# Gate magnitudes from the ratio, and transposes in front of `up` in two row tiles, in a gated linear attention followed by a low-rank mixer

## The chip, the core and the metric

The kernel runs on one core of one Trainium2 chip. A core has a matrix engine (TensorE, PE in the profile, with its weight loads shown apart as PEld), a vector engine (VectorE, DVE), an activation engine (ScalarE, ACT), GpSimd (POOL) and a queue engine (SyncE, SP). They run side by side, each through its own instructions in order, and wait for each other through semaphores. PE writes to PSUM only, and DVE or ACT copy from there. DMA engines move data between the chip's main memory and the core's; here the loads are issued by SP and most of the stores by POOL. The metric is the time of one execution on the device, in microseconds (us); smaller is better.

## The reference

Two stages. The first is a linear attention with complex gates: B = 4 batches, H = 8 heads, S = 768 steps, head size D = 48.

```python
mag = np.sqrt(a_re * a_re + a_im * a_im)
scale = np.minimum(mag, 0.999) / (mag + 1e-06)
a_re_n, a_im_n = (a_re * scale, a_im * scale)
for t in range(S):
    ar, ai = (a_re_n[:, :, t, :, None], a_im_n[:, :, t, :, None])
    new_re = ar * S_re - ai * S_im
    new_im = ar * S_im + ai * S_re
    kv = np.einsum('bhd,bhe->bhde', k[:, :, t], v[:, :, t])
    S_re, S_im = (new_re + kv, new_im)
    y[:, :, t] = np.einsum('bhd,bhde->bhe', q[:, :, t], S_re)
```

Its output, heads side by side (x, 4 x 768 x 384), goes through a mixer: a product of rank 32 over the steps, then two channel products with a hidden size of 1536.

```python
xt = x.transpose(0, 2, 1)
h = xt @ U @ V
u = x + h.transpose(0, 2, 1)
ch = np.maximum(u @ w_ch1, 0.0) @ w_ch2
return (u + ch).astype(np.float32)
```

The weights of the mixer arrive in float64; q, k, v and the gates in float32.

## The kernel before, in words

The steps are cut into 24 chunks of 128 (six for each batch). In a chunk the recurrence becomes products: with the running log magnitude and the running phase of the gates, q and k are weighted by exp and by cosine and sine, and then a masked product within half chunks and a state between them give y.

**Gates.** Two chunks form a group (`GROUPS`, 12 groups of 128 x 768 values; group 0 is done in two parts of 384). `magnitudes_of` (L644) squares both parts of the gate on ACT (L651), adds them with bounds on DVE (L654), keeps a bounded sum (L655), and checks on DVE with two maxima (L657) whether the real part is larger than the imaginary one in size. ACT takes a Ln, an Exp and a Ln (L660 to L662); then the log magnitude with its cap comes either from DVE alone (L665, L667; groups 0 to 2, `SPREAD`) or from an ACT Relu and DVE (L669, L670). From group 3 on (`SPLIT`) the result `GL` is split into two reduced-precision halves `GS` (L676, L677). A second Ln and Exp give one over the magnitude, and its product with the imaginary part (L680) is the ratio whose arc tangent is the angle (after the magnitude's part, L718). `within` (L684) forms the prefix sum over the steps on PE (`es ps`, L691 and L695) and two Exp of it (`es`). `angles` does the same for the phase (`ph`, L755 to L761; the rounding to whole turns is `F`, L763 and L764), `waves` gives cosine and sine (`cs`). Ln and Exp are in one table of ACT, arc tangent and sine in another; a change is a table load (L435).

**Chunks.** `prep` (L793) weights q and k on DVE (L801), multiplies them with `cs` (L805, `QKC`), and turns the result on PE: 16 transposes of 64 rows each, in two row tiles of the array (`tile_position`, L816), whose results ACT copies to `QK` (L822). `chain` (L827) has the inner products (L845), their mask (L848), the state (`dk`, L865) and the output (`y`, L894 and L902), whose copies give `xo` (L911, L913).

**Mixer.** `mixer` (L918) works on pairs of chunks: `rank` (L937), `mixed` (L960), then `turned` (L969): three whole 128 x 128 transposes of u for each chunk (`uTp`, L976) and one copy to `uT`, on DVE for the first chunk of a pair (L982) and on ACT for the second (L980). The first channel product is `up` (L991) for the first two pairs and from the third pair on `up_fewer` (`few`, L1103), a scheme with 15 block products instead of 18. The second is `down` (L1192) for the first pair and `down_two` (L1235, 7 instead of 8 block products) for the others. Stores follow (`leave`, L1179). The weights are turned from float64 into float32 by five steps of DVE or ACT for each block of 768 columns (`single`, L555), with two buffers for the raw words, so the third block is loaded only when the first or the second has been converted.

**What sets the order.** Every step is entered with `plan.add`, which numbers it. The list `ORDER` gives the order in which the numbered steps are issued; each engine's queue has its own steps in that order. `reads` and `writes` of a step only serve to refuse an order in which a step comes before what it needs. `SPARE` names steps in front of which filler matmuls are issued. PSUM has two pools: `psM` with 2 tiles, used by `up`, `down` and parts of `few`, and `psS` with 6 for everything else.

At the end `judge` (L1361) counts on PE whether any of the checks failed; if so, a general version of the kernel runs (`in_general`), which with these inputs it does not.

## Time and profile before

| | |
|---|---|
| time, median of 3 runs | 555.85 us (555.32 to 556.29) |
| profiled execution, from its first to its last instruction | 552.8 us |
| the median less that span: what lies around it | 3.05 us |
| PE busy | 526.9 us (95%) |
| weight loads busy | 477.3 us (86%) |
| DVE busy | 432.8 us (78%) |
| ACT busy | 317.8 us (57%) |
| POOL busy | 32.2 us (6%) |
| read from main memory, written | 33.60 MB, 4.76 MB |

The profile is of one execution, and its time is told as the span alone; the whole time of that execution is not among its rows, so the last line of the three sets it against the median of the runs. "Busy" is the time in which an engine has an instruction in work; PE's instructions overlap, so a busy PE is not yet PE at its peak. In rows by group, the numbers after the bar are the sum of busy time and the mean duration of one instruction in ns, and after the next bar the idle time of the engine in front of them with what ended it. In the chain of waits each line is a piece of the chain that ended last, with its start, its length and what ran.

### The profile page before, as it was taken

The numbers are of one execution on the slowest core, as the hardware profiler recorded it, in microseconds if no ns is written. First come the engines' busy times: TensorE is split into PE (matmuls) and PEld (weight loads), VectorE is DVE, ScalarE is ACT, GpSimd is POOL, SyncE is SP. The second block draws the span as 40 slices with busy tenths as digits, with TensorE's granted clock in tenths as the row PEclk, the third lists the DMA queues.
The fourth block names the chain that finished last, engine by engine and source line by source line (L and its number), as shares of the span: only waits on it lengthen the run. The fifth ranks groups of instructions, "written<-read, shape, count | busy, mean of one in ns | idle before, by whom it ended". The sixth has DMA issues, their size and how long they took to land.

```text
span 552.8 us, 16672 instructions
## 1 busy us (share of the span) xinstructions
PE 526.9 (95%) x7228; PEld 477.3 (86%) x7228; DVE 432.8 (78%) x828; ACT 317.8 (57%) x553; POOL 32.2 (6%) x61
## 2 busy tenths in 40 slices
PE   2899999999999999999999999999999999999996
PEld 1677776767999987999999998999999989999995
DVE  6899989999999987998787987786953635567352
ACT  6889999795597787567827956626512232110100
POOL 1000000001010000102001001002000000000000
PEclk9999999999999999999999999999999999999999
DMA  9988876523441354314513425003300000000001
GB/s 229 187 184 174 195 170 151 144 30 87 88 89 30 56 104 77 59 31 85 91 38 67 74 38 111 2 1 59 59 9 23 17 11 15 8 8 23 21 9 34
DMA packets 150688, 39.92 MB, mean 72 GB/s; under 512 B 145912, under 2 KB 147408, under 8 KB 150608
## 3 DMA queue, kind: packets, MB, share of 16 engines
q1 hardware_dynamic: 148400, 34.43, 31.2%
q0 software_dynamic: 2208, 4.35, 2.3%
q8 instruction: 59, 0.97, 0.7%
q14 instruction: 21, 0.17, 0.1%
HBM read 33.60 MB, written 4.76 MB: 69 GB/s over the span
## 4 chain that ended last, share of the span: by engine, by line
PE 73%; DVE 12%; ACT 4%; issue 2%; DMA 1%; POOL 0%; DVEq 0%; SPq 0%; ACTq 0%; POOLq 0%
PE down L1235 26%; PE few L1103 25%; PE tr L816 4%; PE dk L865 3%; PE inner L845 3%; PE y L902 3%; PE up L991 2%; PE y L894 2%; DVE xo L444 1%; ACT gate L438 1%; PE rank L937 1%; PE ph L755 1%; PE mixed L960 1%; PE uTp L976 1%; PE es ps L691 1%
## 5 line engine op out<-in xcount | busy, mean ns | idle before, releaser
L1111 ACT COPY h<-few 128x512 f32<-128x512 f32 x60 | 35.1, 585 | 87.3 <-PE few L1103 87.1
L1235 PE MATMUL down<-w,h 128*128 128x192 f32 x396 | 72.7, 330 | 0.9 <-DVE xo L444 0.7
L438 ACT ACTIVATE gate<-gate 128x768 f32<-128x768 f32 (+2 forms) x74 | 65.6, 900 | 9.2 <-DVE GS L750 3.8
L1235 PEld LDWEIGHTS down<-w,h 128*128 128x128 f32 x396 | 64.5, 190 | 3.7 <-issue 1.5
L822 ACT COPY QK<-tr 112x512 f32<-112x512 f32 x96 | 49.9, 596 | 17.8 <-PE tr L816 17.7
L444 DVE TENSOR_TENSOR xo<-down,xo 128x192 f32<-128x192 f32 (+1 forms) x79 | 29.9, 385 | 33.9 <-PE down L1235 33.4
L1115 DVE CUSTOM_DVE_ANT_1 h<-few,h 128x512 f32<-128x512 f32 x60 | 40.5, 686 | 15.7 <-PE few L1103 11.8
L1103 PE MATMUL few<-extra,w 128*128 128x128 f32 x400 | 50.9, 276 | 0.0
L1103 PEld LDWEIGHTS few<-extra,w 128*128 128x128 f32 x400 | 48.0, 192 | 0.1
L441 DVE TENSOR_TENSOR QKC<-qk,cs 128x768 f32<-128x768 f32 x48 | 44.4, 950 | 1.7 <-PE dk L865 1.3
L1235 PE MATMUL down<-stage 128*128 128x192 f32 x198 | 37.9, 330 | 0.4 <-DVE xo L444 0.4
L438 ACT ACTIVATE es<-es ps 128x384 f32<-128x384 f32 x48 | 20.1, 502 | 31.2 <-PE es ps L691 29.2
L444 DVE TENSOR_TENSOR h<-few,h 128x512 f32<-128x512 f32 x30 | 20.6, 688 | 20.4 <-ACT h L1111 12.1
L1179 POOL DMA_DIRECT2D out_dram<-xo x32 | 17.9, 558 | 313.8 <-DVE xo L444 297.7
L991 PE MATMUL up<-uT,w 128*128 128x256 f32 x144 | 34.5, 387 | 0.7 <-ACT uT L980 0.7
L1235 PEld LDWEIGHTS down<-stage 128*128 128x128 f32 x198 | 32.3, 190 | 1.7 <-DVE xo L444 1.0
L1103 PE MATMUL few<-gate,w 128*128 128x128 f32 x240 | 32.2, 278 | 0.4 <-DVE gate L1075 0.4
L435 ACT ACT_TABLE_LOAD x24 | 30.8, 1283 | 1.1 <-PEq L1439 0.7
L816 PEld LDWEIGHTS tr<-ident,QKC 64*112 64x112 f32 x768 | 24.2, 130 | 8.3 <-issue 3.6
L816 PE MATMUL tr<-ident,QKC 64*112 64x64 f32 x768 | 28.9, 221 | 2.4 <-DVE QKC L441 2.4
L991 PEld LDWEIGHTS up<-uT,w 128*128 128x128 f32 x144 | 26.4, 190 | 5.3 <-ACT uT L980 0.9
L1103 PEld LDWEIGHTS few<-gate,w 128*128 128x128 f32 x240 | 29.3, 192 | 0.8 <-PE uTp L976 0.6
(161 smaller groups left out, 1100.4 us busy)
## 6 DMA issues: line engine op xcount, KB each, us to landing
stage<-in_moe_w_ch_dram SPq DMA_DIRECT2D x12, 768.0 KB
gate<-in_a_im_dram SPq DMA_DIRECT2D x24, 192.0 KB
gate<-in_a_re_dram SPq DMA_DIRECT2D x24, 192.0 KB
VP<-in_v_dram SPq DMA_DIRECT2D x24, 192.0 KB
qk<-in_q_dram SPq DMA_DIRECT2D x24, 192.0 KB
qk<-in_k_dram SPq DMA_DIRECT2D x24, 192.0 KB
out_dram<-xo POOLq DMA_DIRECT2D x12, 192.0 KB, 2.2
out_dram<-xo POOLq DMA_DIRECT2D x20, 96.0 KB, 2.1
```

Source lines behind the costliest of these rows:

```text
L435: ACT(1.4, rank, lambda: nc.scalar.preload_act_table_set(name), writes=[TABLE])
L438: return nc.scalar.activation(out=o, in_=i, func=f, **kw)
L441: nc.vector.tensor_tensor(out=o, in0=a, in1=b, op=OP.mult)
L444: nc.vector.tensor_tensor(out=o, in0=a, in1=b, op=OP.add)
L816: nc.tensor.transpose(out=get(*ps[r])[0:DQ, h], in_=get(*qkc)[at, h].rearrange("p u d -> p (u d)")[:, 0:DQ], identity=ident[at, at], tile_ ...
L822: nc.scalar.copy(out=get(*QK)[:, u].rearrange("p (h t) -> p h t", t=CH)[:, :, r * HC:(r + 1) * HC], in_=get(*ps[r])[0:DQ])
L991: nc.tensor.matmul(out=get(*ps)[:, e], lhsT=w1[:, f, (ff + e) * 128:(ff + e + 1) * 128], rhs=get(*uT)[:, f], start=(f == 0), stop=(f == KD ...
L1103: nc.tensor.matmul(out=get(*ps)[:, q], lhsT=w()[:, q * 128:(q + 1) * 128], rhs=v[0](), start=(n == 0 and q == 0), stop=True, skip_group_ch ...
L1111: ACT(c_act(n3 * CH) - 0.045, RU, lambda i=i, k=k: nc.scalar.copy(out=at(i, k), in_=get(*ps)), [ps], [o])
L1115: DVE(c_dve(n3 * CH), RU, lambda i=i, k=k: nc.vector._custom_dve(dve_ops.TENSOR_ADD_SAT, out=at(i, k), in0=get(*ps), in1=at(i, k), s0=math ...
L1179: queue.dma_start(out=out[b, c * CH:(c + 1) * CH, lo:hi], in_=get("xo", i)[:, lo:hi])
L1235: nc.tensor.matmul(out=get(*to)[:, part], lhsT=x(j), rhs=y[:, j], start=(first and j == 0), stop=(j == KH - 1), skip_group_check=not first)
```

## The change

There are four parts.

1. For the groups from 1 on (`RATIO`) `magnitudes_of` hands over to a new `ratio_of`. It bounds the real part from below by a tiny number, takes Ln of it and Exp of minus that (one over the real part), multiplies by the imaginary part (the ratio), squares that on DVE with a running maximum (`wide`, the check that the ratio is at most 1 in size), and takes Ln of 1 plus the square. The negative log magnitude is then minus half of this less the Ln of the real part; Exp and Ln for the 1e-6 and the cap follow. Squares, bounded sums, the two maxima and the second Ln and Exp are gone in these groups. The split is moved into a function of its own, unchanged. Group 0 stays as it was.
2. `turned` makes six transposes of 64 rows in two row tiles, into two PSUM tiles, and copies each half on its own, one on DVE and one on ACT. For the last two pairs these PSUM tiles come from the pool `psM`.
3. Reads and writes of some steps in the plan are changed (`w2i`, `bank`, the whole of `y[1]`). They bind the order and add no instruction. `judge` has one more column to reduce, to compare and to count.
4. `ORDER` is another list throughout (2203 steps instead of 2210), and `SPARE` has 31 filler steps instead of 34.

```diff
 SPARE = {
-    125: 2, 135: 10, 199: 14, 209: 1, 223: 5, 243: 2,
+    125: 2, 135: 10, 196: 14, 220: 5,
 }
...
+    RATIO, TINY = 1, 2.0 ** -60
...
-    low = singles.tile([128, GC * DM], FP, name="low")
+    low = singles.tile([128, DM], FP, name="low")
...
-    bad = singles.tile([128, 1 + 2 * NT], FP, name="bad")
+    bad = singles.tile([128, 1 + 2 * GC], FP, name="bad")
     nc.vector.memset(bad, -1.0)
+    wide = singles.tile([128, 1 + NG], FP, name="wide")
+    nc.vector.memset(wide, 0.0)
...
+            if g >= RATIO:
+                ratio_of(lo, hi, t, R1, W, X, L, Y, AR, AI)
+                return
...
+        def ratio_of(lo, hi, t, R1, W, X, L, Y, AR, AI):
+
+
+            ca, cd = c_act(W), c_dve(W)
+            DVE(c_one(W), R1, lambda: nc.vector.tensor_scalar(out=t(l), in0=t(ar), scalar1=TINY, scalar2=None, op0=OP.max), AR, [L])
+            table(ca, R1, lambda: act(t(l), t(l), AF.Ln), [], [L])
+            table(ca, R1, lambda: act(t(x), t(l), AF.Exp, scale=-1.0), [L], [X])
+            DVE(cd, R1, lambda: mul(t(x), t(x), t(ai)), AI, [X])
+            DVE(cd + 0.06, R1, lambda: nc.vector._custom_dve(
+                dve_ops.TENSOR_TENSOR_REDUCE_MULT_MAX, out=t(y), in0=t(x), in1=t(x), s0=-math.inf, s1=1.0,
+                accum_out=wide[:, g:g + 1]), [X], Y + [("wide", 0, g)])
+            table(ca, R1, lambda: act(t(y), t(y), AF.Ln, bias=1.0), [], Y)
+            DVE(cd, R1, lambda: nc.vector.scalar_tensor_tensor(out=t(l), in0=t(y), scalar=-0.5, in1=t(l), op0=OP.mult, op1=OP.subtract), Y, [L])
+            table(ca + 0.09, R1, lambda: act(t(y), t(l), AF.Exp, bias=leps), [L], Y)
+            table(ca, R1, lambda: act(t(y), t(y), AF.Ln, bias=1.0), [], Y)
+            DVE(cd, R1, lambda: nc.vector.scalar_tensor_tensor(out=t(l), in0=t(l), scalar=-LNMAX, in1=t(y), op0=OP.max,
+                                                               op1=OP.add), Y, [L])
+            split(t, R1, L, W)
+            for i in range(lo, hi):
+                within(i, R1, L)
...
-                                                                     in_=get(*y[1])[side(r, 1)]), [y[1] + (r,)], [xi + (r + 1,)])
+                                                                     in_=get(*y[1])[side(r, 1)]), [y[1]], [xi + (r + 1,)])
...
-            psum((nm, k), "M" if nm in ("up", "down") or (nm, k) == ("rank", 0) else "T", shape, padded)
+            late = nm == "uTp" and i0 >= (B - 1) * NCH + MC
+            psum((nm, k), "M" if nm in ("up", "down") or late or (nm, k) == ("rank", 0) else "T", shape, padded)
...
-            tr = out_of("uTp", i, [128, KD, CH], [128, 4, CH])
+            tr = [out_of("uTp", (i, r), [128, KD, HC], [128, H, HC]) for r in range(2)]
 
             def turn():
                 for f in range(KD):
-                    nc.tensor.transpose(out=get(*tr)[:, f], in_=get(*u)[:, f * 128:(f + 1) * 128], identity=ident)
-            PE(0.33, R0, turn, [u], [tr], steps=KD)
-            to = lambda: get(*uT)[:, :, cc * CH:(cc + 1) * CH]
-            if cc:
-                ACT(c_act(DM) - 0.045, R0, lambda: nc.scalar.copy(out=to(), in_=get(*tr)), [tr], [uT + (cc,)])
-            else:
-                DVE(c_dve(DM), R0, lambda: nc.vector.tensor_copy(out=to(), in_=get(*tr)), [tr], [uT + (cc,)])
+                    for r in range(2):
+                        at = slice(r * HC, (r + 1) * HC)
+                        nc.tensor.transpose(out=get(*tr[r])[:, f], in_=get(*u)[at, f * 128:(f + 1) * 128], identity=ident[at, at],
+                                            tile_position=(r * HC, 0))
+            PE(0.2, R0, turn, [u], tr, way=5, steps=2 * KD)
+            for r in range(2):
+                to = lambda r=r: get(*uT)[:, :, cc * CH + r * HC:cc * CH + (r + 1) * HC]
+                if r:
+                    ACT(c_act(KD * HC) - 0.045, R0, lambda to=to, r=r: nc.scalar.copy(out=to(), in_=get(*tr[r])), [tr[r]], [uT + ((cc, r),)])
+                else:
+                    DVE(c_dve(KD * HC), R0, lambda to=to, r=r: nc.vector.tensor_copy(out=to(), in_=get(*tr[r])), [tr[r]], [uT + ((cc, r),)])
...
-                    PE(0.975, RM, lambda half=half: products(half), reads(half) + [("w2s", 0)],
+                    PE(0.975, RM, lambda half=half: products(half), reads(half) + [("w2s", 0), ("w2i", 0)],
                        [to + (part,), ("bank", to[1])], steps=KH)
...
-                DVE(c_dve(DH if y is not None else DM), R0, f, [ps + (part,)] + ([] if also is None else [ps + (also,)]),
+                DVE(c_dve(DH if y is not None else DM), R0, f, [ps + (part,), ("bank", ps[1])] + ([] if also is None else [ps + (also,)]),
...
             nc.tensor.matmul(out=get(*ps)[0:1], lhsT=most, rhs=ones, start=True, stop=False)
+            nc.tensor.matmul(out=get(*ps)[0:1], lhsT=widest, rhs=ones, start=False, stop=False)
             nc.tensor.matmul(out=get(*ps)[0:1], lhsT=least_, rhs=ones[0:DQ], start=False, stop=True)
```

28 lines of the change are left out of this document (16 added, 12 removed), and 168 rows, old and new, of the table ORDER.

## The prediction

> **What bounds the kernel now.** I read the page first: the sums by engine, the slices, the shares of the chain that ended last.
>
> ```profile
> span 552.8 us, 16672 instructions
> PE 526.9 (95%) x7228; PEld 477.3 (86%) x7228; DVE 432.8 (78%) x828; ACT 317.8 (57%) x553; POOL 32.2 (6%) x61
> PE   2899999999999999999999999999999999999996
> PE 73%; DVE 12%; ACT 4%; issue 2%; DMA 1%; POOL 0%; DVEq 0%; SPq 0%; ACTq 0%; POOLq 0%
> ```
>
> TensorE (PE) is busy for 526.9 of 552.8 us and holds 73% of the chain; VectorE (DVE) is the only other engine with a weight in it, 12%. From the fourth slice on, the PE row is nines. So what matters is where PE is not yet, or no longer, full, and what PE itself executes. The table by stage (columns: stretch, its length, then busy time of PE, weight load, DVE, ScalarE (ACT) and GpSimd, each with its count, then clock, DMA share, GB/s) tells where:
>
> ```profile
> 0.00:20.00 20.00, 8.01 (x33) 5.75 (x34) 13.96 (x37) 13.04 (x23) 2.17 (x14) 1.00 1.01 216
> 20.00:40.00 20.00, 17.85 (x361) 14.55 (x361) 20.00 (x34) 18.17 (x32) 0.00 (x0) 1.00 0.93 178
> 40.00:80.00 40.00, 37.44 (x719) 29.75 (x717) 39.97 (x65) 37.05 (x64) 0.00 (x0) 1.00 0.83 184
> 80.00:120.00 40.00, 39.45 (x375) 28.19 (x371) 36.05 (x60) 36.46 (x59) 0.96 (x1) 1.00 0.49 124
> 400.00:440.00 40.00, 39.83 (x515) 38.90 (x508) 21.50 (x39) 10.19 (x21) 1.65 (x3) 1.00 0.08 19
> 540.00:553.00 13.00, 7.78 (x47) 7.18 (x45) 3.39 (x9) 0.00 (x0) 0.00 (x0) 0.92 0.11 36
> ```
>
> PE lacks 12.0 us in the first 20, 2.2 in the next, 2.6 in 40 to 80, and 5.2 at the very end (the last additions and the store, which the change leaves alone). That is 21.9 of the 25.9 us without PE; the 460 us between hold the other 4.0. And from 20 to 80 us DVE has no free time at all (20.00 of 20, 39.97 of 40): there DVE decides when PE gets its operands. The opening is DVE's and the latency of its chain; the rest is PE's own work. The change touches both.
>
> **The gates, groups 1 to 11.** These rows (groups by line and shape: busy us, mean ns of one) price what goes and what comes:
>
> ```profile
> L657 DVE CUSTOM_DVE_ANT_0 low<-gate 128x768 f32<-128x768 f32 x22 | 20.9, 951 | 2.6 <-DMA gate<-in_a_im_dram 2.6
> L657 DVE DVE_READ_ACCUMULATOR2_ANT bad<- 128x1 f32 x26 | 2.1, 82 | 0.0
> L654 DVE CUSTOM_DVE_ANT_0 GL<-gate 128x768 f32<-128x768 f32 x11 | 10.5, 951 | 0.7 <-ACT gate L438 0.7
> L655 DVE SCALAR_TENSOR_TENSOR gate<-gate 128x768 f32<-128x768 f32 x11 | 10.4, 950 | 0.0
> L665 DVE TENSOR_SCALAR GL<-GL 128x768 f32<-128x768 f32 x2 | 1.1, 552 | 0.0
> L670 DVE SCALAR_TENSOR_TENSOR GL<-GL,gate 128x768 f32<-128x768 f32 x9 | 8.5, 950 | 0.9 <-ACT GL L438 0.9
> L438 ACT ACTIVATE gate<-gate 128x1536 f32<-128x1536 f32 x11 | 16.4, 1489 | 5.6 <-DVE GS L750 3.8 <-issue 1.7
> L438 ACT ACTIVATE gate<-gate 128x768 f32<-128x768 f32 x55 | 45.5, 839 | 3.6 <-DMA gate<-in_a_re_dram 2.9 <-DVE gate L655 0.4
> L438 ACT ACTIVATE gate<-GL,leps 128x768 f32<-128x768 f32 x11 | 10.3, 939 | 1.6 <-DVE gate L655 1.6
> L438 ACT ACTIVATE GL<-GL,lmax 128x768 f32<-128x768 f32 x9 | 8.4, 932 | 0.0
> ```
>
> A group from 3 on loses on ACT the squares of both parts (1.49) and the Relu (0.93); its five passes of Ln and Exp stay five. That is 2.4 us, for nine groups 22 us; groups 1 and 2, which have no Relu, lose 1.5 each. On DVE a group from 3 on has L654, L655, two L657 with their accumulator reads (0.08 each) and L670, 4.9 us, replaced by one tensor_scalar (as L665, 0.55), one product with a maximum (as L657, 1.03) and two scalar_tensor_tensor (0.95 each), 3.5 us: 1.4 us less, 9 x 1.4 = 13; groups 1 and 2 give up 2.0 each. From group 3 on I cost this gain at nothing: PE covers it (39.8 of 40 us in 400 to 440, 39.5 in 80 to 120). Without that cover it would be worth at most the 4.0 us above, at least nothing. The price is latency: Ln, Exp, product, product with maximum, Ln, DVE, Exp, Ln, DVE stand strictly one behind the other, where before half of them ran side by side. Groups 1 and 2 feed PE in the opening, so there it counts.
>
> **The opening.** From here on rows of the timeline (start us, us, engine, line):
>
> ```profile
> 20.50 0.95 DVE L657 CUSTOM_DVE_ANT_0 low<-gate 128x768 f32<-128x768 f32 x1
> 21.38 0.95 DVE L588 SCALAR_TENSOR_TENSOR w<-stage,w 128x768 uint32<-128x768 uint32 x1
> 23.58 0.95 DVE L654 CUSTOM_DVE_ANT_0 GL<-gate 128x768 f32<-128x768 f32 x1
> 24.45 1.82 DVE L441 TENSOR_TENSOR QKC<-qk,cs 128x768 f32<-128x768 f32 x2
> 22.00 0.62 ACT L438 ACTIVATE cs<-cs,quarter 128x384 f32<-128x384 f32 x1
> 40.35 1.49 ACT L438 ACTIVATE gate<-gate 128x1536 f32<-128x1536 f32 x1 [1.70 <-issue]
> 25.45 0.66 PE L816 MATMUL tr<-ident,QKC 64*112 64x64 f32 x16 [1.65 <-DVE QKC L441]
> 32.47 0.91 PE L695 MATMUL es ps<-GL,prefix_r 128*128 128x384 f32 x2
> 45.03 4.15 PE L991 MATMUL up<-uT,w 128*128 128x256 f32 x18 [0.66 <-ACT uT L980]
> ```
>
> Numbering the operations as the code adds them gives each number of the two lists ORDER a name. Four steps follow.
> (1) The first weighted q and k (24.45) stands in DVE's queue behind two whole steps of group 1 (20.50 with its read, 23.58: 2.0 us) and the last two steps of the second w1 conversion (one of them at 21.38); in the new list only a 0.55 us maximum of group 1 and none of these four. DVE is then ready some 3 us earlier, and the cosine it reads (22.00) comes earlier too, as the squares of group 1 no longer stand in ACT's queue (1.5 us). The limit becomes that cosine, at about 21.5, so the transposes of 25.45 start near 22.7.
> (2) Group 1's prefix sum (32.47) takes no part in that gain: table load over near 24.0, Ln and Exp to 25.6; the ratio waits for DVE's queue until 26.1 and with its square lasts to 28.0; Ln to 28.9; DVE to 29.8; Exp and Ln to 31.7; DVE to 32.7. PE waits there for about a us, with 1.1 us of later work already done.
> (3) From there to the first `up` (45.03) the old order needs 12.6 us. ACT runs the 1.49 us of squares for group 2 at 40.35 ahead of the rounding on which the phases wait; without them, and with `es` of both chunks issued at once, I add the same steps to about 10 us. But the third w1 block is loaded only when DVE has finished the second: at about 31.2 now, before at 22.3 (the end of 21.38). Two rows of the page, the transfers:
>
> ```profile
> stage<-in_moe_w_ch_dram SPq DMA_DIRECT2D x12, 768.0 KB
> out_dram<-xo POOLq DMA_DIRECT2D x20, 96.0 KB, 2.1
> ```
>
> 768 KB at the 178 GB/s of 20 to 40 us are 4.4 us, with some 2 us to the landing as for the stores 37.6; its five conversion steps, with 1 us of other work between, end at 41.6. First `up`: 42 to 43 instead of 45.03.
> (4) Up to the next prefix sums the same PE operations follow in both lists, so a lead of 2.4 us stays; bounds 0 (step 2 later by as much) and 3.1 (the load in time).
> To these, 0.4 us for the 2.6 us that PE lacks in 40 to 80, with DVE's work ahead of chunk 5's masked copy some 6 us smaller, by the same durations added along both lists; bounds 0 and 2.
>
> **The transposes in front of `up`.** The chain of waits, 244 to 276 us (start, length, what), shows what an operation takes when PE is the limit:
>
> ```profile
> 244.47 0.33 PE uTp L976 x3
> 251.99 0.89 PE few L1103 x8
> 266.08 1.04 PE tr L816 x32
> 267.12 1.09 PE few L1103 x8
> L982 DVE COPY uT<-uTp 128x384 f32<-128x384 f32 x12 | 6.6, 550 | 3.3 <-PE uTp L976 3.3
> L980 ACT COPY uT<-uTp 128x384 f32<-128x384 f32 x12 | 5.7, 479 | 11.5 <-PE uTp L976 11.3
> L444 DVE TENSOR_TENSOR xo<-down,xo 128x192 f32<-128x192 f32 x66 | 22.8, 352 | 29.7 <-PE down L1235 29.4
> L911 ACT COPY xo<-y 128x192 f32<-128x192 f32 x24 | 7.6, 318 | 1.5 <-PE y L902 1.1
> ```
>
> Three whole transposes take 0.33 us. The prep transposes already run in two row tiles: 32 of them in 1.04, two by two, 0.065 a pair. Three pairs: 0.20 us, 0.13 less, 24 times: 3.1 us. But eight products take 0.89 between others of their shape (251.99) and 1.09 between a row-tiled block and one in quadrants (267.12): PE pays 0.20 for two changes of tile shape at that operation alone, and the neighbours pay a part; I take 0.17 for a change. In the two lists neighbouring PE operations differ in tile shape 168 times before and 179 times after (the new transposes are put beside others in row tiles where possible): 11 x 0.17 = 1.9 us more. Net 1.2 us less; bounds 3.1 less (changes free) and 1.2 more (three pairs 0.30, with one more edge of 0.10 on top). Each chunk's one copy becomes two of half the size, on DVE and ACT at once: like the 0.35 and 0.32 us of the last two rows, so about 1.9 us more on each engine in all, hidden behind PE, and `up` can start 0.2 us earlier; taken as 0. Each takes two of the PSUM tiles instead of one; the last four take both of the other pool, with a product in between: 0, at most 0.4 each.
>
> **The rest.** The added dependency and the whole-tile reads bind only the order, no instruction: 0. In SP's queue five transfers of gates and v that stood ahead of chunk 0's q and k stand behind them; by their bytes at the 216 GB/s of the first stage all land before steps 1 and 2 need them: 0, bounds -0.5 and 1. POOL's stores change places with the carries: POOL has nothing to do for 94% of the time: 0, at most 0.5. The final verdict gets three small DVE steps and two small matmuls, in PE's queue before the last products: 0.3 at most, taken as 0.1. Three filler pairs fewer are inside the opening.
> Sum: -2.4 - 0.4 - 1.2 + 0.1 = -3.9, a span of 548.9. The profiled execution lies 3.05 us below the median of 555.85 by its span; with the same around it, 551.9 us.
>
> **Rivals.** Below, 0.2% (1.1 us) is what a measurement can tell from no change.
> Slower: the serial gate chain. It passes six times between DVE and ACT, both full in 20 to 40 (20.00 and 18.17 of 20), and a hand-over that meets a running 0.9 us instruction waits up to that. Groups 1 and 2 are in front of PE one after the other; if each comes 2 us later than I add, the 3.9 are gone; with 3 us the time is 558. For it: step 2 leaves no slack. Against: the list puts only short work between the steps. 0.14.
> The opening gains nothing, since the third w1 block comes later still and holds `up`: only the transposes are left, -1.1, 554.7. For it: its buffer is freed 10 us later. 0.15, half of it within 0.2%.
> More: the 13 and 22 us that DVE and ACT save close what PE lacks after 40 us too (2.6 + 4.0, say 3.4 of them): 548.5. Against: most of these are spots of under 0.5 us. 0.14.
> PSUM: the row tiles hold two tiles each of a pool of six, and a transpose waits for a copy. If half of one 0.60 us QK copy is added for each of the 24, 7.2 us come on top: 559. 0.04.
>
> ```profile
> L822 ACT COPY QK<-tr 112x512 f32<-112x512 f32 x96 | 49.9, 596 | 17.8 <-PE tr L816 17.7
> ```
>
> The Trainium skill, TensorEngine Tiling (Array Packing), section Restrictions and Gotchas, warns of just that: row tiles write to different PSUM banks, so row tiling raises the pressure on PSUM; the trace shows no queue there yet, since ACT idles for 17.7 us before these copies, waiting for PE.
> The change does not do what it says: the halves do not overlap at 128 columns, 6 x 0.065 = 0.39, +4.6 on the sum: 556.5. The prep rows speak against it. 0.03.
>
> **How the numbers follow.** Forecast 0.50; the rest as above. Faster: 0.50 + 0.14 + half of 0.15 = 0.72. Same: the other half and 0.03 = 0.10. Slower: 0.14 + 0.04 = 0.18. The forecast's own range is 550.2 to 553.6 (bounds of the opening and the transposes). The range for 8 in 10 takes in the larger gain and the lost opening and a part of the slower cases: 547.8 to 557.0.
>
> **What would show it.** First prep transposes near 22.7 us, group 1's prefix sum near 32.7, first `up` near 42.5; PE's stages from 80 on as full as now; three pairs of transposes at 0.17 to 0.31 us; ACT's busy sum near 295 and DVE's near 418. Wrong, if PE waits over 2 us for GL of group 1 or 2, if `up` waits for w1, or if PE waits for the copies of uT.

## The result, and the profile after

| | before | after |
|---|---|---|
| time, median | 556.07 us (555.32 to 556.82) | 550.18 us (548.04 to 550.73) |
| profiled execution, first to last instruction | 552.8 us | 548.5 us |
| PE busy | 526.9 us | 524.2 us |
| DVE busy | 432.8 us | 419.6 us |
| ACT busy | 317.8 us | 297.3 us |

The changed kernel takes 0.9887 of the time before, 95% interval 0.9866 to 0.9908: 5.9 us less by the medians, 4.3 us less by the two profiled executions. The changed kernel's profiled execution (550.73 us, mean granted clock 0.991) is the longest of its four; the others have a clock of 0.994. The forecast was 551.9 us in a range from 547.8 to 557.0.

The head of the page of the changed kernel: span, busy sums, PE by slices, its clock, and the shares of the chain.

```profile
span 548.5 us, 16738 instructions
PE 524.2 (96%) x7296; PEld 473.6 (86%) x7296; DVE 419.6 (77%) x819; ACT 297.3 (54%) x545; POOL 32.0 (6%) x61
PE   2889989999999999999999999999999999999996
PEclk9999997999999999999999999999999999999999
PE 82%; DVE 9%; ACT 4%; DMA 3%; issue 2%; SPq 0%; DVEq 0%; ACTq 0%; POOLq 0%
```

PE's share of the chain went from 73% to 82% and DVE's from 12% to 9%. New is a 7 in the row of the clock, in the seventh slice: TensorE was granted less than its full clock there. The table by stage (columns as in the prediction) shows five of the stretches again:

```profile
0.00:20.00 20.00, 8.45 (x39) 6.10 (x40) 14.37 (x38) 13.46 (x25) 2.17 (x14) 1.00 0.90 204
20.00:40.00 20.00, 17.09 (x424) 14.40 (x422) 19.30 (x31) 18.08 (x33) 0.00 (x0) 1.00 0.74 150
40.00:80.00 40.00, 39.17 (x783) 30.91 (x777) 38.49 (x62) 38.29 (x69) 0.00 (x0) 1.00 0.97 199
80.00:120.00 40.00, 38.20 (x244) 26.66 (x245) 32.97 (x54) 30.73 (x50) 0.96 (x1) 0.91 0.59 130
400.00:440.00 40.00, 39.82 (x763) 38.17 (x762) 27.10 (x55) 16.34 (x34) 3.00 (x5) 1.00 0.16 37
```

From 40 to 80 us PE lacks 0.8 us, where it lacked 2.6. From 80 to 120 it lacks 1.8, where it lacked 0.6, and there the mean clock is 0.91 where it was 1.00. The opening, in rows of the timeline of PE and DVE:

```profile
22.74 1.11 PE L846 MATMUL tr<-ident,QKC 64*112 64x64 f32 x32
21.27 1.82 DVE L442 TENSOR_TENSOR QKC<-qk,cs 128x768 f32<-128x768 f32 x2
32.62 1.53 PE L725 MATMUL es ps<-GL,prefix_r 128*128 128x384 f32 x4 [1.03 <-DVE GL L700]
41.64 2.55 PE L1026 MATMUL up<-uT,w 128*128 128x256 f32 x11
54.83 1.45 PE L725 MATMUL es ps<-GL,prefix_r 128*128 128x384 f32 x4
```

The first weighted q and k (21.27, before 24.45) and the first prep transposes (22.74, before 25.45) come 2.7 to 3.2 us earlier, group 1's prefix sum (32.62, before 32.47) comes no earlier, the first `up` (41.64, before 45.03) 3.4 us earlier. The next group's prefix sum starts at 54.83; the same operation started at 57.67 before. The transposes in front of `up`, by group, first in the kernel before, then after with their copies:

```profile
L976 PE MATMUL uTp<-ident,xo 128*128 128x128 f32 x72 | 11.4, 277 | 0.4 <-DVE xo L444 0.3
```

```profile
L1009 PE MATMUL uTp<-ident,xo 64*128 64x64 f32 x144 | 8.1, 234 | 0.0
L1017 DVE COPY uT<-uTp 128x192 f32<-128x192 f32 x24 | 8.1, 350 | 2.8 <-PE uTp L1009 2.8
L1015 ACT COPY uT<-uTp 128x192 f32<-128x192 f32 x24 | 7.1, 318 | 20.6 <-PE uTp L1009 20.6
```

PE is busy with them for 8.1 us instead of 11.4. Counted from the start of each of the 24 operations to the start of the next one on PE, they take 6.1 us instead of 10.3. Of the 10.3, 1.3 are idle time behind three of them, in which PE waited for another engine; without it they took 9.1, so the operations themselves save 3.0 us.

What the prediction didn't have stands at 79 us. Timeline of PE, and then the stretches around it:

```profile
78.90 0.55 PE L924 MATMUL y<-VP,AT 64*64 64x48 f32 x21
81.67 0.66 PE L924 MATMUL y<-VP,AT 64*64 64x48 f32 x11 [2.22 <-issue]
```

```profile
78.00:80.00 2.00, 1.45 (x55) 1.27 (x51) 1.77 (x3) 1.92 (x5) 0.00 (x0) 1.00 1.18 252
80.00:82.00 2.00, 0.34 (x10) 0.34 (x11) 1.93 (x4) 0.87 (x2) 0.00 (x0) 0.90 0.63 108
82.00:84.00 2.00, 2.00 (x43) 1.91 (x35) 2.00 (x3) 0.00 (x0) 0.00 (x0) 0.50 0.05 13
84.00:86.00 2.00, 2.00 (x13) 0.67 (x12) 0.16 (x1) 1.67 (x4) 0.00 (x0) 0.50 0.59 108
86.00:88.00 2.00, 2.00 (x6) 1.43 (x5) 0.97 (x2) 0.96 (x2) 0.00 (x0) 0.50 1.06 357
88.00:90.00 2.00, 2.00 (x14) 0.81 (x12) 0.54 (x1) 0.60 (x2) 0.00 (x0) 0.89 0.14 27
```

In the middle of 32 equal matmuls PE stops for 2.22 us, and the profile names no engine that it waits for ("issue"). Then its clock is at half from 81.62 to 88.44 us, 6.83 us by the clock's own records. So 2.2 us are lost at once and up to 3.4 us by the clock: up to 5.6 us of what had been gained until then.

### The profile page after: what moved, and what is told of

It reads as the page before. It is cut to its first block, busy times and chain, and to the rows that moved or that the text cites. A ratio compares the mean times of both kernels' runs of the same rounds, so it can differ in the third digit from the quotient of the medians.

```text
span 548.5 us, 16738 instructions
## 1 busy us (share of the span) xinstructions
PE 524.2 (96%) x7296; PEld 473.6 (86%) x7296; DVE 419.6 (77%) x819; ACT 297.3 (54%) x545; POOL 32.0 (6%) x61
## 4 chain that ended last, share of the span: by engine, by line
PE 82%; DVE 9%; ACT 4%; DMA 3%; issue 2%; SPq 0%; DVEq 0%; ACTq 0%; POOLq 0%
PE down L1270 28%; PE few L1138 23%; PE dk L895 4%; PE inner L875 4%; PE y L932 4%; PE tr L846 4%; PE y L924 2%; PE up L1026 2%; DMA gate<-F 2%; PE rank L968 2%; PE mixed L991 2%; ACT gate L439 1%; PE uTp L1009 1%; PE es ps L721 1%; PE es ps L725 1%
## 5 line engine op out<-in xcount | busy, mean ns | idle before, releaser
L852 ACT COPY QK<-tr 112x512 f32<-112x512 f32 x96 | 51.4, 593 | 35.3 <-PE tr L846 35.2
L445 DVE TENSOR_TENSOR h<-few,h 128x512 f32<-128x512 f32 x30 | 20.6, 689 | 34.5 <-PE few L1138 22.1
L439 ACT ACTIVATE gate<-gate 128x768 f32<-128x768 f32 (+1 forms) x52 | 40.7, 792 | 11.3 <-DVE wide L693 7.8
L1214 POOL DMA_DIRECT2D out_dram<-xo x32 | 19.6, 645 | 191.1 <-DVE xo L445 159.5
L771 POOL DMA_DIRECT2D gate<-F x15 | 12.1, 805 | 303.2 <-DVE F L794 166.2
L895 PE MATMUL dk<-VP,QKC 64*48 64x48 f32 (+1 forms) x1408 | 27.6, 217 | 1.1 <-issue 1.1
```

The source lines that it names most:

```text
L439: return nc.scalar.activation(out=o, in_=i, func=f, **kw)
L445: nc.vector.tensor_tensor(out=o, in0=a, in1=b, op=OP.add)
L852: nc.scalar.copy(out=get(*QK)[:, u].rearrange("p (h t) -> p h t", t=CH)[:, :, r * HC:(r + 1) * HC], in_=get(*ps[r])[0:DQ])
L895: nc.tensor.matmul(out=get(*dk[r])[x:end, h], lhsT=get(*ks)[at, h, x // DP, 0:end - x], rhs=get(*VPi)[at, h], start=True, stop=True, tile_ ...
```

## The experiments

Ratios are to the kernel before, run on the same chip. Differences to the changed kernel are differences of ratios times 555.85 us; as each ratio is known to about 0.002, such a difference is known to about 1.6 us. Orders are shown in words, with a minus for the old and a plus for the new; the edits themselves exchange step numbers in `ORDER`.

### The pause at 79 us

PE's instructions arrive by DMA: the page has a queue of its own for them. Transfers of the changed kernel by queue:

```profile
q8 instruction: 59, 0.97, 0.8%
```

59 transfers, 16.4 KB each; PE has 7296 matmuls and as many weight loads, so there is one transfer for about 247 of them. The transfers at 72.24 and 79.14 us lie 439 of PE's instructions apart. The later one landed at 80.26, and PE went on at 81.67. The first theory was that the loads hold it up: from 72 to 80 us SyncE issues 1.3 MB of loads, and the DMA share in 78 to 80 is 1.18.

**gate_loads_later.** SyncE's order, two of the loads (a_im 9 and a_im 8) moved back:

```diff
-w2[2], a_im 9, a_re 8, a_im 8, w2[4], v 6, w2[6]
+w2[2], a_re 8, w2[4], v 6, a_im 9, a_im 8, w2[6]
```

> The changed kernel, with the two transfers of the imaginary gates of group 4 issued behind those of the third w2 block and of v for chunk 6 instead of ahead of them (some 8 us later). In the changed kernel's trace PE stops at 79.45 us for 2.2 us without waiting for any engine, and its granted clock is 0.5 from 81.6 to 88.4 us. Theory A: the DMA engines are full with loads from 71 to 79 us, so PE's next 16 KB of instructions, due at about 76 us, come at 79.1; the pause then lowers the clock. A expects the pause under 0.5 us, the clock at 1.0 there, and 2.2 + 3.4 = 5.6 us less than the changed kernel: 544 to 546 us, ratio to the kernel before 0.979 to 0.983. Theory B: the pause belongs to this place of the program (a boundary of an instruction block), whatever is loaded: unchanged, 550 us, ratio 0.989. Theory C: the pause goes and the clock falls all the same: 2.2 us less, 548 us.

Measured: 548.26 us, ratio 0.9857 (0.9837 to 0.9877). The pause stayed, at 2.21 us, and the transfer still began at 79.34. Only one window of half clock followed (83.80 to 87.21). So theory A's pause under 0.5 us was missed, and B's unchanged time too; two loads of 192 KB were too few to tell.

**loads_after_short.** Nothing is issued from 73 to 84 us:

```diff
-v 5, q 6, k 6, a_re 9, w2[2], a_im 9, a_re 8, a_im 8, w2[4], v 6, w2[6]
+v 5, w2[2], w2[4], q 6, k 6, v 6, a_re 9, a_re 8, a_im 9, a_im 8, w2[6]
```

> The changed kernel with six loads of 192 KB (q and k of step 6, both halves of the gates of groups 4) issued behind the conversion block w2[4] instead of ahead of it, and the block w2[2] ahead of where they stood; two VectorE steps that read them stand later. Between 73 and 84 us no load is issued. Theory backlog (the 2.2 us pause of PE at yin5 comes from PE's instruction fetch, which waits behind full DMA engines): the fetch that landed at 80.3 us starts at 76 to 77, the pause is under 0.5 us, the clock stays at 1.0 through 80 to 90, and the time falls by 4 to 5.6 us against the changed kernel: 544.6 to 546.2, ratio to the kernel before 0.980 to 0.983. Theory short instructions (PE goes through some 400 short matmuls and weight loads in 6 us, faster than the next 256 instructions are asked for and come, whatever the DMA does): the fetch still starts after 78 us, the pause is 1.5 us or more, at least one window of half clock follows, ratio 0.985 to 0.990.

Measured: 550.3 us, ratio 0.9919 (0.9896 to 0.9942). Stretches (their last column but two is the clock), and two rows of PE's timeline:

```profile
76.00:78.00 2.00, 2.00 (x83) 1.93 (x80) 2.00 (x4) 2.00 (x4) 0.00 (x0) 1.00 0.03 8
80.00:82.00 2.00, 1.81 (x51) 1.48 (x51) 1.97 (x3) 1.40 (x4) 0.00 (x0) 1.00 0.04 8
96.00:98.00 2.00, 1.96 (x4) 1.26 (x5) 1.98 (x6) 0.62 (x2) 0.00 (x0) 0.50 1.01 370
```

```profile
80.19 0.43 PE L924 MATMUL y<-VP,AT 64*64 64x48 f32 x11 [0.41 <-issue]
96.04 1.28 PE L785 MATMUL ph<-GS,prefix_r 128*128 128x384 f32 x2 [2.86 <-DVE GS L779]
```

With the DMA engines all but idle (share 0.03) the transfer began at 77.88 instead of 79.14, the pause shrank from 2.22 to 0.41 us, and the clock stayed at 1.00 there. Counted from PE's step into the block of instructions before, the transfer began 1.5 us later here and 3.3 us later in the changed kernel. So the backlog of loads had held the transfer, but not for all of its lateness: neither theory is right alone. The time came out no better, and outside both expectations. The gates of group 4 now land late; DVE waits 2.95 us for one, PE waits 2.86 us for what DVE makes of it (until 96.04), and two windows of half clock begin in that wait (94.46 to 101.28). The price was moved, not saved.

**up_between_short.** From tr5 at 73 us to yb5 PE has nothing but short matmuls; here a half of an `up` product (1.5 us) moves in between, and the ACT copy that frees its PSUM tile goes three steps ahead:

```diff
-yin4, inner5, yb4, yin5, yb5, rank0.1, up0.10 (second half), rank0.2
+yin4, inner5, up0.10 (second half), yb4, yin5, yb5, rank0.1, rank0.2
```

> The changed kernel with one half of an up product (three matmuls of 256 columns, about 1.5 us of PE) moved from behind yb5.1 to between yin4 and inner5, into the middle of the run of short matmuls, and the ScalarE copy that frees its PSUM buffer three steps ahead; the loads are as in the changed kernel. If PE stops because it reaches the end of its fetched instructions before the late fetch lands (both theories, backlog and short instructions), PE reaches that place 1.5 us later and the pause falls from 2.2 to about 0.7 us, the clock falls for at most one window, and the time is 1.7 to 5 us under the changed kernel: ratio 0.980 to 0.986. If the pause is tied to the matmuls of yin5 and not to the fetch, it stays at 2.2 us and the ratio at 0.987 to 0.990.

Measured: 545.92 us (545.33 to 546.02), ratio 0.9839 (0.9817 to 0.9861).

```profile
78.00:80.00 2.00, 2.00 (x37) 1.83 (x36) 1.53 (x4) 1.97 (x3) 0.00 (x0) 1.00 1.26 257
80.00:82.00 2.00, 2.00 (x66) 1.61 (x65) 1.86 (x3) 0.69 (x3) 0.00 (x0) 1.00 0.72 100
80.00:120.00 40.00, 39.47 (x305) 27.48 (x304) 37.23 (x58) 34.29 (x56) 1.72 (x2) 1.00 0.57 130
```

No pause here, and the clock is at 1.00 from 16.5 to 542 us. The transfer began at 79.19, as late as in the changed kernel, and landed at 80.47, but PE had come only 331 instructions since the last one instead of 439. It reached the instruction in front of which the changed kernel stops at 81.76, 1.29 us after the landing: just late enough, where a pause of 0.7 us was expected to be left. This version beats both kernels; by the profiled executions the pause and its clock had cost 4.6 us (548.5 to 543.9), by the ratios 2.7.

In all eight kernels with such a pause of 0.4 us or more behind yin4 or, in tiles_old_order, at 163 us, PE goes on 1.30 to 1.53 us after a late transfer has landed (80.26 to 81.67 in the changed one). A count of PE's records (matmuls, weight loads and the sequencer's own) shows where it stops. From 14 us on, the traces of twelve of the thirteen kernels have 20 pauses of 0.3 us or more with no engine named, and each of them stands behind 193 instructions plus a whole multiple of 256: behind 2497 in all seven kernels that stop behind yin4. With these blocks of 256 and the transfers numbered alike, no block in any of the thirteen kernels begins sooner than 1.1 us after its transfer has landed. So B was right about the place, a boundary between blocks, and A about a part of the lateness. That the pause is the wait for instructions is shown; the request itself is in no record.

The kernel before has such pauses too, short ones without half clock. Two rows of its timeline:

```profile
138.51 0.67 PE L865 MATMUL dk<-VP,QKC 64*64 64x48 f32 x31 [0.30 <-issue]
200.86 0.78 PE L865 MATMUL dk<-VP,QKC 64*48 64x48 f32 x21 [0.47 <-issue]
```

PE goes on 1.39 and 1.50 us after a transfer of instructions has landed. The changed kernel has a second one as well, of 0.89 us at 315 us, and up_between_short one of 0.58 at 311.

### The transposes

**whole_new_order.** The changed kernel with whole transposes, three for each chunk. The steps, their order, the two PSUM tiles and the two copies stay: DVE copies two of the three, ACT one.

```diff
-            tr = [out_of("uTp", (i, r), [128, KD, HC], [128, H, HC]) for r in range(2)]
+            tr = [out_of("uTp", (i, r), [128, 2 - r, CH], [128, 4, CH]) for r in range(2)]
...
```

> The changed kernel with whole 128 x 128 transposes in front of up again, in the new order: two of the three go to the PSUM tile that DVE copies, one to the tile that ACT copies, so the steps, the order, the PSUM tiles and the copying engines stay. Changes of tile shape on PE fall from 179 to 171. By the terms of the prediction: 24 x 0.13 = 3.1 us more for the transposes, 8 x 0.17 = 1.4 less for the changes: 1.7 us slower than the changed kernel, about 552 us, ratio to before 0.992. If a change of tile shape costs nothing, 3.1 slower, 553.3 us; if the row tiles bring nothing, no difference.

Measured: 551.58 us, ratio 0.9926 (0.9907 to 0.9946), as the terms of the prediction had it (0.992). The row tiles are worth 0.0039 in the new order, 2.2 us, with an interval from 0.6 to 3.8. On PE the whole transposes take 9.2 us instead of 6.1, and all of PE's work, idle time left out, is 1.5 us longer. The pause at 79 us is there too (3.00 us), so it isn't the row tiles that bring it.

**tiles_old_order.** The kernel before with the row-tiled `turned` alone, in the old order:

```diff
-            tr = out_of("uTp", i, [128, KD, CH], [128, 4, CH])
+            tr = [out_of("uTp", (i, r), [128, KD, HC], [128, H, HC]) for r in range(2)]
...
```

> The kernel before with the row-tiled transposes alone, in the old order. The old order puts them between whole products, so changes of tile shape rise from 168 to 195. By the terms of the prediction: 24 x 0.13 = 3.1 us saved, 27 x 0.17 = 4.6 us paid: 1.5 us slower than before, ratio 1.003. If a change of tile shape costs nothing: 3.1 us faster, ratio 0.994. If the row tiles do not run side by side, 5 us slower or more.

Measured: 562.66 us, ratio 1.0143 (1.0122 to 1.0163), where at most 1.003 was expected. A row of PE's timeline:

```profile
165.54 0.49 PE L818 MATMUL tr<-ident,QKC 64*112 64x64 f32 x9 [1.90 <-issue]
```

Again a pause for instructions, elsewhere: the transfer began at 163.03, 463 of PE's instructions after the one before, and PE went on 1.53 us after it had landed. Of the 7.3 us by which the span grew, 2.7 are there behind this pause, which is 1.9 of them, and 5.1 at the last `down`, with another such pause of 0.7 us at 404.9 on the way. The other 2.1 lie behind the start of the last addition (6.9 us to the end of the span, before 4.8), and why that tail grew isn't settled. The tiling itself cost what it was priced at: with 195 changes of tile shape in the order instead of 168, PE's work, idle time left out, is 1.8 us longer, where 1.5 were expected. The transposes save 0.6 us, `few` and `down` take 1.1 and 1.3 more. What the expectation lacked is the pauses, the waits and the tail.

### The gates

Four kernels have one form of the gates in the other's order. The new steps were put by hand at the places of the old ones (or the reverse), as near as a step's inputs allow, and transposes are whole in the two kernels in the old order and row-tiled in the two in the new. The edit of the form, for the first, against the changed kernel:

```diff
-    RATIO, TINY = 1, 2.0 ** -60
+    RATIO, TINY = (1, 2), 2.0 ** -60
...
-            if g >= RATIO:
+            if g in RATIO:
```

**gates_1_2_old_order.**

> The kernel before with the ratio form of the gates in groups 1 and 2 alone, in the old order: each new step stands at the place of an old one of its engine. Theory of the prediction: the opening is bound by DVE's work and by the squares in ACT's queue, so the lead of 2.4 us comes from these two groups (4.0 us less on DVE, 3.0 less on ACT): 1 to 3 us faster, ratio 0.995 to 0.998, less than with an order of its own. Rival: the chain of these groups is longer from end to end (six hand-overs instead of three), and the prefix sums of groups 1 and 2 come later: 0 to 4 us slower, ratio 1.000 to 1.007.

Measured: 565.58 us, ratio 1.0179 (1.0165 to 1.0194). PE's waits for one operation (in all, times, longest), and a row of its timeline:

```profile
PE tr L846 <- DVE QKC L442: 6.3, 4, 3.6
```

```profile
34.76 1.62 PE L725 MATMUL es ps<-GL,prefix_r 128*128 128x384 f32 x2 [0.41 <-DVE GL L700]
```

That is above both ranges. Group 1's prefix sum is 2.3 us later than before, PE waits 6.3 us for weighted q and k, and behind or within the waits the clock falls to half, from 31.6 to 38.5 and from 62.4 to 69.2 us. That is the prediction's slower rival (a serial chain handed back and forth between two full engines), at the place where it put it, and the half clock on top.

**old_gates_1_2_new_order.** The reverse:

```diff
-    RATIO, TINY = 1, 2.0 ** -60
+    RATIO, TINY = (3, 4, 5, 6, 7, 8, 9, 10, 11), 2.0 ** -60
```

> The changed kernel in its order with the old form of the gates (both squared, the ratio behind the prefix sum) in groups 1 and 2 alone; the old steps stand at the places of the new ones, the squares behind the gates' loads. The prediction gave the ratio form of these two groups the whole gain of the opening, 2.4 us, and 0.4 us up to 80 us. Theory form (the ratio form is what lets the opening be earlier): the group's prefix sum comes later than 32.6 us by 2 us or more, the first up after 43.5 us instead of 41.64, and the time is 1.5 to 4 us over the changed kernel: ratio to the kernel before 0.991 to 0.996. Theory order (the opening gains by which loads, transposes and up stand first, and either form of the gates fits it): the first up within 1 us of 41.64 and the ratio at 0.986 to 0.990.

Measured: 559.06 us, ratio 1.0063 (1.004 to 1.0086), over the range that either theory gave.

```profile
31.42 1.10 PE L847 MATMUL tr<-ident,QKC 64*112 64x64 f32 x16 [4.44 <-DVE QKC L443]
73.44 1.65 PE L792 MATMUL ph<-F,ident 128*128 128x384 f32 x2 [2.99 <-DVE F L795]
```

Group 1's prefix sum comes at 35.6 us (32.62), the first `up` at 45.3 (41.64), and half clock comes with both waits shown, one window from 31.45 and two from 72.41. With the steps placed as they were here, it is the ratio form that lets this order start early, and the old order doesn't let the ratio form gain.

**gates_3_11_old_order.** The kernel before with the same tuple as in the last one:

> The kernel before with the ratio form of the gates in groups 3 to 11 alone, whole transposes, and the old order: each new step of a gate stands at the place of an old one. The prediction costed these groups at nothing, since 22 us of ScalarE and 13 us of VectorE work go away beside a PE that is the bound. By it: ratio 0.997 to 1.003. Rival (the longer serial chain of a gate, maximum, two logarithms and three exponentials one after the other between ScalarE and VectorE, comes late for its group's prefix sum when the order isn't made for it, as it did in groups 1 and 2 alone): ratio 1.006 or more, and PE waits for GL, GS or QKC.

Measured: 579.84 us, ratio 1.0457 (1.0433 to 1.048), 25 us slower. PE's waits, and then DVE's at the new steps (in all, times, longest):

```profile
PE down L1264 <- DVE xo L444: 5.4, 5, 3.8
PE few L1132 <- DVE extra L1104: 3.9, 2, 3.5
PE y L923 <- DVE AT L877: 3.1, 2, 2.4
```

```profile
DVE gate L441 <- ACT gate L438: 6.0, 6, 1.6
DVE GL L696 <- ACT gate L438: 2.0, 4, 0.9
DVE GL L699 <- ACT gate L438: 1.7, 2, 1.2
```

At the three steps of the chain where DVE takes over from ACT it waits 9.7 us; in the changed kernel the same three waits sum to 1.7. What stands behind them in DVE's queue comes late by it, PE waits in many places for additions, masks and copies that were hidden before, and there are three windows of half clock (of 3.41 us each, which cost up to half of that). How the 25 us divide among these wasn't tried.

**old_gates_3_11_new_order.** The changed kernel with the ratio form in groups 1 and 2 alone:

> The changed kernel in its order with the old form of the gates in groups 3 to 11 alone, the old steps at the places of the new ones; some loads of gates stand later, since the old form holds their buffers longer. ScalarE has about 22 us and VectorE about 13 us more to do. The prediction costed these groups at nothing. By it, if the new order's lead hides the old form as well: ratio 0.986 to 0.992. Rival (VectorE and ScalarE of the order are set so that the old form's work comes late for prefix sums, additions and copies, as the new form did in the old order, where it took 25 us): ratio 1.00 or more, and PE waits for GS, QKC, xo or uT.

Measured: 584.01 us, ratio 1.0524 (1.0495 to 1.0554), 35 us over the changed kernel.

```profile
DVE GL L661 <- ACT gate L440: 13.6, 8, 3.6
PE down L1271 <- DVE xo L446: 8.6, 5, 3.2
```

DVE waits 13.6 us for ACT's squares, PE waits 8.6 us for additions, and six windows of half clock (up to 10 us lost) lie between 152 and 361 us. In this kernel and the one above the rival held. These four mix a form with an order not made for it, so none of them prices a form by itself; the next two keep the order.

### What slack DVE and ACT have

**scalar_work_added** and **vector_work_added.** The changed kernel in its own order; in groups 3 to 11 some passes are repeated on the same operands: the two exponentials on ACT in the one, the maximum (in the same way) and the squared ratio on DVE in the other.

```diff
-            table(ca, R1, lambda: act(t(x), t(l), AF.Exp, scale=-1.0), [L], [X])
+            table(ca, R1, lambda: [act(t(x), t(l), AF.Exp, scale=-1.0) for _ in range(1 + (g >= 3))], [L], [X])
...
-            table(ca + 0.09, R1, lambda: act(t(y), t(l), AF.Exp, bias=leps), [L], Y)
+            table(ca + 0.09, R1, lambda: [act(t(y), t(l), AF.Exp, bias=leps) for _ in range(1 + 2 * (g >= 3))], [L], Y)
```

```diff
-                dve_ops.TENSOR_TENSOR_REDUCE_MULT_MAX, out=t(y), in0=t(x), in1=t(x), s0=-math.inf, s1=1.0,
-                accum_out=wide[:, g:g + 1]), [X], Y + [("wide", 0, g)])
+                dve_ops.TENSOR_TENSOR_REDUCE_MULT_MAX, out=t(y), in0=t(x), in1=t(x), s0=-math.inf, s1=1.0,
+                accum_out=wide[:, g:g + 1]) for _ in range(1 + (g >= 3))], [X], Y + [("wide", 0, g)])
...
```

> The changed kernel, its order untouched, with ScalarE's work of the late gates put back in amount: in groups 3 to 11 the first exponential runs twice and the second one three times, with the same inputs and outputs (27 more passes of 128 x 768 at 0.85 to 0.94 us, 25 us in all); each gate's chain is 2.7 us longer for it. The prediction costed the 22 us that go from ScalarE in these groups at nothing. By it: 0.986 to 0.992, the same as the changed kernel. Rival (with the order as it is, ScalarE's time in these stretches is on the way to the copies and exponentials that PE waits for): ratio 1.000 or more, that is 6 us or more of the 25 seen in the span.

> The changed kernel, its order untouched, with VectorE's work of the late gates put back in amount: in groups 3 to 11 the maximum and the squared ratio run twice, with the same inputs and outputs (18 more passes, 9 of 0.55 and 9 of 0.95 us, 13.5 us in all); each gate's chain is 1.5 us longer for it. The prediction costed the 13 us that go from VectorE in these groups at nothing. By it: 0.986 to 0.992. Rival (VectorE, which is busy for most of each stretch, is next to the bound, and its additions come later for PE): ratio 0.995 or more, that is 3.5 us or more of the 13.5 seen in the span.

Measured: 559.95 us, ratio 1.0095 (1.0074 to 1.0116) with 23.4 us of ACT work by the busy sums; 557.15 us (553.27 to 559.13), ratio 1.003 (1.0003 to 1.0056) with 13.6 us of DVE work. The rival held in both. That is 11.6 and 7.9 us over the changed kernel by the ratios and 9.3 and 5.8 by the profiled executions, so two to three fifths of the work, though ACT is busy for 54% of the span and DVE for 77%. Rows of PE's timeline, two of each:

```profile
112.61 4.54 PE L1227 MATMUL down<-w,extra 128*128 128x384 f32 x8 [2.59 <-ACT h L439]
142.08 3.19 PE L1270 MATMUL down<-w,h 128*128 128x192 f32 x18 [2.16 <-ACT h L439]
```

```profile
140.36 3.19 PE L1270 MATMUL down<-w,h 128*128 128x192 f32 x18 [0.70 <-ACT h L439]
244.51 2.22 PE L1270 MATMUL down<-stage 128*128 128x192 f32 x12 [1.16 <-DVE xo L445]
```

Between 60 and 545 us PE's waits of over 0.2 us for other engines sum to 9.6 us in the first and 6.4 in the second, where the changed kernel has 0.7; its pauses for instructions sum to 2.1 and 1.8, in the changed kernel to 3.1. The waits account for most of the longer spans, and the longest of them are over 2 us: work is late at single places, however idle the engine is elsewhere. Whether a full queue does it or the longer chain of each gate (2.7 and 1.5 us, as the expectations say) these two kernels don't separate.

## Why the prediction was right

The time, its side and its range held, and so did the steps of the opening but for the limit in step 3. The sum held less well than the total: gains too small by more than 5 us and a loss that no term had nearly cancelled, so the close total is in good part luck. Counted by equal work (an estimate: each of PE's operations taken at its mean time in the kernel before, fillers left out), the changed kernel is 5.0 us ahead where the pause begins at 79 us (2.8 forecast), 0.5 behind at 88.5, where the full clock is back, and 4.2 ahead at 500 us. So the -3.9 of the sum met -5.0, +5.5 and -4.8, where the last had been put at about -1.1.

- **Step 1** (prep transposes near 22.7 us, since four DVE steps and the squares leave the queue ahead): 22.74. Right.
- **Step 2** (group 1's prefix sum near 32.7, no gain, PE waits about 1 us there): 32.62, 1.03 us of wait. Right.
- **Step 3** (first `up` at 42 to 43): 41.64. Right, a little short, but not by the limit it names: the conversion of the third w1 block ended at 40.4 instead of 41.6, and PE came to `up` from other work without idle time, so it didn't wait for w1.
- **Step 4** (a lead of 2.4 us stays): 2.8 us at the next prefix sums. Right.
- **The 0.4 us for 40 to 80 us**: too small. PE's lack fell from 2.6 to 0.8 us. The first stage and this one together gave 5.0 us up to 79, not 2.8. The gain was in the bounds (0 and 2), the value taken was at the wrong end.
- **The transposes, -1.2 us**: about right, as far as the runs can tell. The operations themselves save 3.0 us where 3.1 were added up. The whole transposes in the new order (eight changes of shape fewer) cost 2.2 us more, where the same terms gave 1.7. What a change of shape costs the neighbours came out lower than set down: 2.4 us for 27 changes in tiles_old_order, 0.09 each instead of 0.17.
- **Missing: the pause and the half clock**, 5.5 us by the count above, 4.6 by the profiled executions with and without it, 2.7 by the ratios. No step and no rival had it, since the sum looked at waits for engines and transfers of data. Of half clock the profile of before shows none between the second slice and the last, but it does show the pauses, 0.30 and 0.47 us. These rows would have warned, with the new order lining up some 400 short instructions in a row, in a stretch with the DMA engines full. Without the pause the prediction would have been too high: up_between_short, 546.9 us by its ratio, lies below the range.
- **Gates from group 3 on at nothing, "PE covers it"**: as a gain, near enough: from 90 to 510 us PE lacked 3.9 us before and lacks 2.1 now (rows below), and no run tells how much of these 1.8 us is theirs. They are a part of the 4.8 us gained behind the pause; the rest is PE's own work, the transposes among it, and its parts stay open. As a reason it was wrong: busy sums don't say that work is covered. Like amounts put back cost 11.6 and 7.9 us. A gain was bounded by the 4.0 us that PE lacked; a loss has no such bound. The two rows, first before and then after, in stretches of the same bounds:

```profile
90.00:510.00 420.00, 416.06 (x5663) 383.45 (x5658) 335.88 (x653) 236.10 (x412) 28.38 (x44) 1.00 0.26 52
```

```profile
90.00:510.00 420.00, 417.86 (x5748) 384.30 (x5747) 325.74 (x647) 219.81 (x407) 26.07 (x40) 1.00 0.27 53
```

- **The rivals**: the slow serial chain isn't in the changed kernel (1.03 us of wait at group 1, none at group 2), but it is real: in the old order it costs 10 us for groups 1 and 2. "The opening gains nothing" fell with step 3. "More" came true in size: PE's lack fell by 1.7 us from 40 to 80 us and by 1.8 from 90 to 510, 3.5 against the 3.4 that it named, but the pause hid it; whether the smaller loads of DVE and ACT brought it or the order, no run separates. PSUM pressure: no wait of PE in the changed kernel names the copies of uT, whose engines wait 2.8 and 20.6 us for PE instead (rows L1017 and L1015); the rule of the Trainium skill (TensorEngine Tiling (Array Packing), Restrictions and Gotchas) that row tiles raise that pressure shows no price here. In tiles_old_order PE does wait 0.9 us for such a copy in front of `up`, where it waited 0.7 before. The halves overlap: the two of a pair start 3 to 9 ns apart on PE, and three pairs take 0.19 to 0.33 us, not the 0.39 of halves one after the other.
- **The 3.05 us around the span**: too much. In 39 other executions of the kernel before it is 1.75 to 1.93 us, in the four of the changed kernel 1.9 to 2.2; the profiled execution was simply shorter than the median. So the span was forecast to 0.4 us (548.9 and 548.5), the time to 1.7. The forecast's own range, 550.2 to 553.6, isn't the sum of the bounds that the text names for it, and 550.18 lies at its lower edge.
- ACT's busy sum is 297.3 (about 295 forecast), DVE's 419.6 (about 418).

What carries the result is the pair, not a part: the new form in the old order loses 10 us (groups 1 and 2) and 25 us (3 to 11), the row tiles there 8 us, and the old form in the new order 10 and 35 us. The prediction read both lists step by step, so it priced the pair. What each part would bring in an order made for it alone no run shows.

## What to carry to other kernels

Where an order is written by hand, price an edit together with the order that it comes with; busy sums of 54% and 77% hid only about half of 23 and 14 us more. Removing work from an engine that isn't the bound gains at most what the bound lacks, adding the same work can cost half of it. Look in PE's rows for waits that name no engine, however short, and in a long row of short matmuls count the instructions and look at the DMA share: one longer product put in between was worth about as much here (2.7 us) as the whole tiling of the transposes (2.2).

## What the runs showed of the hardware

- **PE can run out of instructions.** Twelve kernels, the one before among them, show pauses of 0.30 to 3.00 us with no engine named, all at the boundary of a block of 256 instructions; PE goes on 1.2 to 1.8 us after the block's transfer of 16.4 KB has landed. Without loads beside it the transfer came 1.3 us earlier.
- **A short pause can halve the clock for whole windows.** Between the opening and the end half clock came in pieces of 3.41 or 6.83 us, and how long a pause is doesn't tell whether it comes: it came with one of 1.33 us (scalar_work_added, 82.9 to 86.3) and not with waits of 2.16 (scalar_work_added, 142.1) or 2.65 us (old_gates_3_11_new_order, 105.7). Where the pause lies does. Cut the time since the full clock began into windows of 3.41 us: in the thirteen traces all 13 windows in which PE is idle for more than 1.9 us end in half clock, none of those with less than 1.27 us does, and of the 18 between 6 do. The wait of 2.16 us lies across an edge, with 0.96 us before it and 1.20 behind; the changed kernel's 2.22 lies within one window (78.20 to 81.62). The Trainium skill (TensorE: Matmul & The Clock Gate, HAM oscillation — how this bites in real kernels) asks for no PE gaps over some 3.4 us. That bound is too loose here: 2.22 us brought two windows. The length of the free-running window that the Trainium skill gives (the same page, What's actually happening) agrees with the 3.41 us here.
- **Tile shapes.** An operation that takes 0.89 us among its like took 1.09 between two others; three pairs of transposes in row tiles took 0.19 us among row tiles and 0.33 between other shapes (by their starts in the changed kernel). The Trainium skill (TensorEngine Tiling (Array Packing), Key Properties) says that changing the mode drains TensorE and gives no price; here it is about 0.1 us a change for a whole-array operation and 0.05 to 0.1 for the transposes.
